# A quad's partial sums kept in one PSUM bank and copied out by ScalarE, instead of added on VectorE

## The chip, the cores and the metric

The kernel runs on one core of a Trainium2 chip. The metric is the device time of one execution in microseconds (us). The engines are TensorE (PE in the rows, its weight loads PEld), VectorE (DVE), ScalarE (ACT), GpSimd (POOL) and SyncE (SP, which issues the loads and stores).

## The reference

Three blocks follow one another on a sequence of 768 tokens, 2 batches and 512 features, all in fp32:

```python
state = gamma * state + einsum(k[t], v[t]);  y[t] = scale * einsum(q[t], state)
u  = x + (xt @ U @ V).T;      x2 = u + relu(u @ w_ch1) @ w_ch2
h  = relu(x2 @ w_in);         u, v = split(h);   v_n = layernorm(v)
out = (u * (w_spatial @ v_n + b)) @ w_out
```

The first block is a linear attention with decay (8 heads of 64), the second a low-rank token mix and an MLP of width 2048, the third a gated MLP of width 1024 with a 768 x 768 mix over tokens.

## The kernel before, in words

Every fp32 operand is split into two fp32r tiles, a high and a low part, and each product of two operands is three matmuls (`triple`, L640). The stages, by the time of the profile: attention and token mix up to about 70 us; the first MLP up to about 322 us, in eight steps of two hidden tiles (its first two steps by plain products, tiles `c`, the other six by quads), whose second products go to tiles `acc`; the gate half of the third block (`gate_u`, quads `qu`) to 345 us; its value half with the norm (`gate_v`, quads `qv`) to 381 us; the token mix (tiles `pz`) to 427 us; the output product (`final`, quads `qo`) to 457 us.

A **quad** (L653) computes a 2 x 2 block product by seven products instead of eight. `PRODUCTS` (L320) names their operands 1 to 7; sums and differences of operands (`s1`, `t1` and so on) are made beforehand. Each of the seven is two triples, that is six matmuls, of 384 columns (first MLP, `gate_u`) or 256 columns (`gate_v`, `final`). With P1 to P7 for the products, the four outputs are

```
out00 = P1 + P2             out10 = P1 + P6 + P7 + P4
out01 = P1 + P6 + P5 + P3   out11 = P1 + P6 + P7 + P5
```

There are 28 quads: 12 in the first MLP (m = 2 to 7, two batches, tiles `q20` to `q71`), 4 `qu`, 6 `qv` and 6 `qo`. Before, a quad takes four PSUM banks of the eight: `qa` collects P1 and then P2, `qb` P6, `qc` P7 and then P4, `qd` P5 and then P3. P1 is copied to an SBUF tile y1 (L667, shown as L457, on ScalarE or VectorE), VectorE adds P6 to it (L668) and makes y2 = P7 + y1 (L670). `store` then adds y1 or y2 to the bank for three of the outputs, on VectorE (L730, L769, L786 or L849), and takes out00 straight from `qa`. In the first MLP `store` goes on with a relu on ScalarE (L731), the high part (L732) and the low part (L733).

No order is written out by hand. Each operation goes to a planner (`Plan`, L44) with a key, its dependences, its tiles and its cost on each engine that may take it (`aps`, `vps` and others, from L263). The planner fills the engines' queues by time (`arrange`, L93); for PE it takes what can start first. The only instruction it does not cost is the load of ScalarE's function table, which is put ahead of the first square root of the norm (L797). PE, VectorE and ScalarE each run their own queue in order.

A matmul that writes a bank anew, or adds to it, waits until the reads of that bank that stand before it are done. In the rows a wait shows as idle time ahead of the instruction, of PEld in PE's case.

## Time and profile before

| what | value |
|---|---|
| median of 3 runs | 462.59 us (462.5 to 462.69) |
| span of the profiled execution, first to last instruction | 460.2 us |
| granted TensorE clock over it | 1.000 |
| PE / VectorE / ScalarE / POOL busy | 455.8 / 408.6 / 258.1 / 104.1 us |
| DMA, mean | 94 GB/s |

The profiled execution is given by its span alone; no total of its own is listed. The span lies 2.4 us under the median of the runs. Busy times are sums over the span; whether an engine's idle time costs anything is seen in the waits and in the timeline.

### The profile page before, as it was taken

The numbers are of one execution on the slowest core, as the hardware profiler recorded it, in microseconds if no ns is written. First come the engines' busy times: TensorE is split into PE (matmuls) and PEld (weight loads), VectorE is DVE, ScalarE is ACT, GpSimd is POOL, SyncE is SP. The second block draws the span as 40 slices with busy tenths as digits, with TensorE's granted clock in tenths as the row PEclk, the third lists the DMA queues.
The fourth block names the chain that finished last, engine by engine and source line by source line (L and its number), as shares of the span: only waits on it lengthen the run. The fifth ranks groups of instructions, "written<-read, shape, count | busy, mean of one in ns | idle before, by whom it ended". The sixth has DMA issues, their size and how long they took to land.

```text
span 460.2 us, 8518 instructions
## 1 busy us (share of the span) xinstructions
PE 455.8 (99%) x3258; PEld 446.2 (97%) x3258; DVE 408.6 (89%) x867; ACT 258.1 (56%) x532; POOL 104.1 (23%) x99
## 2 busy tenths in 40 slices
PE   9999999999999999999999999999999999999997
PEld 6898899999999999999999999999999999999997
DVE  2969999999999999999789788899998899989943
ACT  3667676475556656566355444557657878443410
POOL 3164333433323221321131012101310001240000
PEclk9999999999999999999999999999999999999999
DMA  8996212141422233334112112100004220000042
GB/s 309 399 400 240 93 45 93 32 153 47 136 94 91 93 93 108 120 93 139 46 58 81 47 46 70 35 1 0 2 0 139 93 91 1 1 2 1 0 180 95
DMA packets 14727, 43.34 MB, mean 94 GB/s; under 512 B 1760, under 2 KB 2400, under 8 KB 14688
## 3 DMA queue, kind: packets, MB, share of 16 engines
q1 hardware_dynamic: 14544, 42.80, 27.0%
q8 instruction: 25, 0.41, 0.4%
q14 instruction: 14, 0.11, 0.1%
q10 hardware_dynamic: 144, 0.02, 0.0%
HBM read 39.67 MB, written 3.15 MB: 93 GB/s over the span
## 4 chain that ended last, share of the span: by engine, by line
PE 99%; DVE 0%; issue 0%
PE acc L336 29%; PE pz L336 11%; PE c L336 7%; PE x L336 5%; PE sc L336 3%; PE g L336 1%; PE t L470 1%; PE ds L336 1%; PE idle L336 1%; PE hu L336 1%; PE qu11c L336 0%; PE q40a L336 0%; PE qu11d L336 0%; PE qu11a L336 0%; PE qu01d L336 0%; PE qu01c L336 0%
## 5 line engine op out<-in xcount | busy, mean ns | idle before, releaser
L336 PE MATMUL acc<-a,hw 128*128 128x384 f32 x512 | 130.2, 334 | 0.0
L336 PEld LDWEIGHTS acc<-a,hw 128*128 128x128 f32 x512 | 92.5, 188 | 0.3 <-DVE a L733 0.3
L336 PE MATMUL acc<-a,lw 128*128 128x384 f32 x256 | 85.5, 334 | 0.0
L758 DVE TENSOR_TENSOR x<-acc,x 128x384 f32<-128x384 f32 x128 | 69.6, 550 | 7.0 <-PE acc L336 6.8
L565 POOL TENSOR_TENSOR rw<-rw,tw 128x512 int32<-128x512 int32 x32 | 43.9, 1374 | 112.7 <-DVE rw L564 102.1
L336 PEld LDWEIGHTS acc<-a,lw 128*128 128x128 f32 x256 | 48.1, 188 | 0.0
L731 ACT ACTIVATE y<-y 128x384 f32<-128x384 f32 x36 | 18.9, 524 | 39.3 <-DVE y L730 39.2
L561 ACT ACTIVATE yw<-raww 128x512 f32<-128x512 f32 x32 | 21.6, 678 | 16.7 <-DVE rw L564 16.6
L564 DVE SCALAR_TENSOR_TENSOR rw<-yw,rw 128x512 uint32<-128x512 uint32 x32 | 24.2, 759 | 0.0
L733 DVE TENSOR_TENSOR a<-y,a 128x384 fp32r<-128x384 f32 x36 | 21.0, 585 | 2.7 <-ACT a L732 2.4
L562 ACT ACTIVATE tw<-raww 128x512 int32<-128x512 uint32 x32 | 21.5, 673 | 2.0 <-POOL rw L565 2.0
L422 DVE SCALAR_TENSOR_TENSOR pt<-sc,scales,shared 128x384 f32<-128x384 f32 x21 | 11.9, 611 | 8.3 <-PE sc L336 8.2
L732 ACT CAST a<-y 128x384 fp32r<-128x384 f32 x36 | 18.5, 514 | 1.1
L336 PE MATMUL pz<-hws,vn 128*128 128x384 f32 x72 | 19.1, 335 | 0.0
L336 PE MATMUL pz<-ws,vn 128*128 128x384 f32 x108 | 19.0, 334 | 0.0
L336 PEld LDWEIGHTS pz<-ws,vn 128*128 128x128 f32 x108 | 18.8, 188 | 0.0
L563 DVE TENSOR_SCALAR rw<-yw 128x512 uint32<-128x512 uint32 x32 | 18.3, 582 | 0.1
L565 POOL TENSOR_TENSOR rwo<-rwo,two 128x512 int32<-128x512 int32 x4 | 5.2, 1294 | 54.8 <-DVE rwo L564 54.8
L574 DVE TENSOR_TENSOR lw<-rw,hw 128x512 fp32r<-128x512 f32 x20 | 17.1, 855 | 0.0
L336 PE MATMUL c<-f00b,hw 128*128 128x384 f32 x64 | 16.4, 338 | 0.0
L336 PE MATMUL c<-f01b,hw 128*128 128x384 f32 x64 | 16.2, 334 | 0.0
L573 ACT CAST hw<-rw 128x512 fp32r<-128x512 f32 x20 | 12.4, 619 | 6.2 <-POOL rw L565 5.8
(1090 smaller groups left out, 1293.8 us busy)
## 6 DMA issues: line engine op xcount, KB each, us to landing
raww<-in_w SPq DMA_DIRECT2D x32, 512.0 KB, 3.5
q<-in_qT SPq DMA_DIRECT2D x8, 384.0 KB, 8.0
k<-in_kT SPq DMA_DIRECT2D x8, 384.0 KB, 8.0
kk<-in_k SPq DMA_DIRECT2D x8, 384.0 KB, 8.0
v<-in_v SPq DMA_DIRECT2D x8, 384.0 KB, 7.9
out_y<-out SPq DMA_DIRECT2D x11, 256.0 KB, 2.1
raws<-in_ws SPq DMA_DIRECT2D x6, 384.0 KB, 2.9
rawwu<-in_wu SPq DMA_DIRECT2D x4, 512.0 KB, 3.8
```

The lines of the kernel that those rows point to most:

```text
L336: nc.tensor.matmul(o, l, r, start=start, stop=stop, skip_group_check=True)
L561: op({"A": c}, lambda E: E.activation(y.t, words(1).bitcast(F32), AF.Copy, scale=2.0 ** -112), r=whole, w=[y])
L562: op({"A": c}, lambda E: E.activation(t.t, words(0), AF.Copy, scale=2.0 ** -29), r=whole, w=[t])
L563: op({"V": vone(n)}, lambda E: E.tensor_single_scalar(r.t, y.t.bitcast(U32), 3, ALU.logical_shift_left), r=[y], w=[r])
L564: op({"V": vss(n)}, lambda E: E.scalar_tensor_tensor(r.t, y.t.bitcast(U32), 0x80000000, r.t, ALU.bitwise_and, ALU.bitwise_or), r=[y, r], w ...
L565: op({"G": gss(n)}, lambda E: E.tensor_tensor(r.t.bitcast(I32), r.t.bitcast(I32), t.t, ALU.add), r=[r, t], w=[r])
L573: op({"A": acp(DM)}, lambda E: E.copy(h.t, f(r.t)), r=[r], w=[h])
L574: op({"V": vss(DM), "G": gss(DM)}, lambda E: E.tensor_sub(l.t, f(r.t), f(h.t)), r=[r, h], w=[l])
L731: op({"A": (525, False)}, lambda E: E.activation(y[0](), y[0](), AF.Relu), r=[y[1]], w=[y[1]])
L732: op({"A": acp(T)}, lambda E: E.copy(t.t[:, 0, :], y[0]()), r=[y[1]], w=[(t, 0)])
L733: op({"V": vss(T), "G": gss(T)}, lambda E: E.tensor_sub(t.t[:, 1, :], y[0](), f(t.t[:, 0, :])), r=[y[1], (t, 0)], w=[(t, 1)])
L758: op({"V": vps(T)}, lambda E, o=o, v=xs(b, d, h): E.tensor_add(v, o.t, v), r=[o, ("X", b, d, h)], w=[("X", b, d, h)])
```

## The change

The seven products are put in the order 1 2 6 5 7 4 3 (they stood in the order 1 5 6 7 2 4 3). Products 1, 6, 7 and 4 all go to `qa`, one on top of the other, so that the bank holds P1, then P1 + P6, then P1 + P6 + P7, then out10. After each of the first three ScalarE copies the bank to an SBUF tile (y for 1, 6 and 7; the first of them may also go to VectorE). Product 2 has `qb`, products 5 and 3 have `qd`; `qc` is gone. `store` adds y(1) to `qb`, y(7) and y(6) to `qd`; out10 needs no addition and is read from `qa`. Where `ys2` gives two SBUF tiles (256 columns), the copy of 7 takes the tile of the copy of 1.

```diff
--- before.py
+++ after.py
@@ -305,7 +305,7 @@
 STEP0, STEP1, UV = 5.0, 5.0, 20.0
 LOADS = "q0 k0 q1 k1 U V0 q2 k2 V1 q3 k3 w10 w11 q4 k4 w20 w21 q5 k5 q6 k6 q7 k7".split()
 LEAD = 10.0
-ORDER = '1567243'
+ORDER = '1265743'
 LAST = "b11 b21 t1=b12-b11 t1 t2=b22-t1 t2 t3=b22-b12 t3 t4=b21-t2 t4 b22"
 LASTSUMS = "t1=b12-b11 t1 t2=b22-t1 t2 t3=b22-b12 t3 t4=b21-t2 t4"
 SUM0, SUM1 = 80.0, 80.0
@@ -655,27 +655,22 @@
 
 
 
-        qa, qb, qc, qd = (bank([P, n], f"q{name}{x}") for x in "abcd")
-        y1, y2, y3 = ys()
-        done = set()
+        qa, qb, qd = (bank([P, n], f"q{name}{x}") for x in "abd")
+        ys = dict(zip("167", ys()))
         for x in order:
             plan.key += STEP[n] * plan.pace
-            done.add(x)
-            product({"1": qa, "6": qb, "7": qc, "5": qd, "2": qa, "4": qc, "3": qd}[x], PRODUCTS[x], x in "1675")
-            if x == "1":
-                op({"A": aps(n), "V": vps(n)}, lambda E: cpy(E, y1[0](), qa.t), r=[qa], w=[y1[1]])
-            elif x == "6":
-                op({"V": vps(n)}, lambda E: E.tensor_add(y1[0](), qb.t, y1[0]()), r=[qb, y1[1]], w=[y1[1]])
-            elif x == "7":
-                op({"V": vps(n)}, lambda E: E.tensor_add(y2[0](), qc.t, y1[0]()), r=[qc, y1[1]], w=[y2[1]])
-            elif x == "2":
-                store(0, 0, qa)
+            product({"1": qa, "6": qa, "7": qa, "4": qa, "2": qb, "5": qd, "3": qd}[x], PRODUCTS[x], x in "125")
+            if x in ys:
+                y = ys[x]
+                op({"A": aps(n), "V": vps(n)} if x == "1" else {"A": aps(n)}, lambda E, y=y: cpy(E, y[0](), qa.t), r=[qa], w=[y[1]])
+            if x == "2":
+                store(0, 0, qb, ys["1"], ys["1"])
             elif x == "4":
-                store(1, 0, qc, y1, y3)
+                store(1, 0, qa)
             elif x == "3":
-                store(0, 1, qd, y1, y1)
-            if x in "57" and {"5", "7"} <= done:
-                store(1, 1, qd, y2, y2)
+                store(0, 1, qd, ys["6"], ys["6"])
+            if x == "7":
+                store(1, 1, qd, ys["7"], ys["7"])
 
     def ys3(name):
         def get():
@@ -686,7 +681,7 @@
     def ys2(name):
         def get():
             bs = [Buf("st", [P, DM // 2], F32, f"y{name}{x}") for x in range(2)]
-            return [(lambda z=z: bs[z].t[:], bs[z]) for z in (0, 1, 1)]
+            return [(lambda z=z: bs[z].t[:], bs[z]) for z in (0, 1, 0)]
         return get
 
     def own(x):
```

The planner makes new queues of this. The three places below are quoted with the semaphores waited for in brackets (`Activation` is ScalarE's).

**PE, a quad of the first MLP** (`q40`; `acc` are the second products of the step before). Before, ahead of product 4 (the rows `q40c<-...qw`): one product of the other bank and one `acc`.

```order
L336 MATMUL q40a<-f00b_722,hw14a 128x384
L336 MATMUL q40a<-f00b_722,lw14a 128x384
L336 MATMUL q40a<-f00b_733,hw14a 128x384 x2
L336 MATMUL q40a<-f00b_733,lw14a 128x384
L336 MATMUL acc_2580<-a_2480,hw_1960 128x384 [waits DVE_49]
L336 MATMUL acc_2580<-a_2480,hw_1960 128x384
L336 MATMUL acc_2580<-a_2480,lw_1992 128x384
L336 MATMUL acc_2580<-a_2406,hw_1990 128x384 x2
L336 MATMUL acc_2580<-a_2406,lw_2004 128x384
L336 MATMUL q40c<-f00t_1266,qw_2121 128x384 [waits DVE_49]
L336 MATMUL q40c<-f00t_1266,qw_2121 128x384 x2
L336 MATMUL q40c<-f00t_1316,qw_2121 128x384 x3
```

Now, from the last rows of product 7 (`hsbw`, `lsbw`) to product 4 (`qw`), both in `q40a`:

```order
L336 MATMUL q40a<-f00t_1228,lsbw_2147 128x384
L336 MATMUL q40a<-f00t_979,hsbw_2137 128x384 x2
L336 MATMUL q40a<-f00t_979,lsbw_2147 128x384
L336 MATMUL acc_2586<-a_2489,hw_1946 128x384 x2
L336 MATMUL acc_2586<-a_2489,lw_1958 128x384
L336 MATMUL acc_2586<-a_2435,hw_1994 128x384 x2
L336 MATMUL acc_2586<-a_2435,lw_2008 128x384
L336 MATMUL q40a<-f00t_1264,qw_2091 128x384 [waits Activation_49]
L336 MATMUL q40a<-f00t_1264,qw_2091 128x384 x2
L336 MATMUL q40a<-f00t_1416,qw_2091 128x384 x3
L336 MATMUL acc_2609<-a_2489,hw_1946 128x384 [waits DVE_49]
L336 MATMUL acc_2609<-a_2489,hw_1946 128x384
```

Product 4 stood three groups of six matmuls behind product 7 (an `acc`, product 2, an `acc`) and waited for VectorE; it stands one group behind it and waits for ScalarE.

**PE, the last quad of the program** (`qo12`, 256 columns). Before, product 7 (end of it), product 2 and the start of product 4:

```order
L336 MATMUL qo12c<-lsbwo_5267,f21t_5369 128x256
L336 MATMUL qo12c<-hsbwo_5257,f21t_5369 128x256
L336 MATMUL qo12a<-hwo0a,f21b_5177 128x256 [waits Activation_49]
L336 MATMUL qo12a<-lwo0a,f21b_5177 128x256
L336 MATMUL qo12a<-hwo0a,f21b_5177 128x256
L336 MATMUL qo12a<-hwo1a,f21b_5208 128x256
L336 MATMUL qo12a<-lwo1a,f21b_5208 128x256
L336 MATMUL qo12a<-hwo1a,f21b_5208 128x256
L336 MATMUL qo12c<-qwo_4988,f21t_5362 128x256 [waits DVE_49]
L336 MATMUL qo12c<-qwo_4988,f21t_5362 128x256 x2
```

Now, product 7, product 4 and the start of product 3:

```order
L336 MATMUL qo12a<-hsbwo_5008,f21t_5307 128x256 [waits Activation_49]
L336 MATMUL qo12a<-lsbwo_5017,f21t_5307 128x256
L336 MATMUL qo12a<-hsbwo_5008,f21t_5307 128x256
L336 MATMUL qo12a<-hsbwo_5236,f21t_5354 128x256
L336 MATMUL qo12a<-lsbwo_5245,f21t_5354 128x256
L336 MATMUL qo12a<-hsbwo_5236,f21t_5354 128x256
L336 MATMUL qo12a<-qwo_4966,f21t_5347 128x256 [waits Activation_49]
L336 MATMUL qo12a<-qwo_4966,f21t_5347 128x256 x2
L336 MATMUL qo12a<-qwo_5173,f21t_5383 128x256 x3
L336 MATMUL qo12d<-hsbwo_5008,f21b_5286 128x256 [waits DVE_49]
L336 MATMUL qo12d<-lsbwo_5017,f21b_5286 128x256
```

Product 4 follows product 7 in the same bank with nothing between them.

**ScalarE, the second quad of `gate_v`** (`qv01`). Before, around the load of the function table:

```order
L457 COPY yv_4361<-qv01a 128x256 [waits PE_49,Activation_49]
L787 ACTIVATE r_4339<-qv00d 128x256 [waits DVE_49]
L635 CAST hws_4375<-raws_4321 128x384 [waits DMAHW3_49]
L635 CAST ws_4382<-raws_4321 128x384
L797 ACT_TABLE_LOAD
L797 ACTIVATE sm_4359<-sm_4359 128x2 [waits DVE_49]
L635 CAST ws_4401<-raws_4348 128x384 [waits DMAHW4_49]
L787 ACTIVATE r_4409<-qv01a 128x256 [waits PE_49]
L787 ACTIVATE r_4419<-yv_4399 128x256 [waits DVE_49]
```

Now:

```order
L782 ACTIVATE r_4344<-qv00d 128x256 [waits DVE_49]
L782 ACTIVATE r_4381<-qv01b 128x256 [waits DVE_49]
L457 COPY yv_4388<-qv01a 128x256 [waits PE_49]
L457 COPY yv_4398<-qv02a 128x256 [waits PE_49,Activation_49]
L792 ACT_TABLE_LOAD
L792 ACTIVATE sm_4359<-sm_4359 128x2 [waits DVE_49]
L457 COPY yv_4337<-qv01a 128x256 [waits PE_49]
L782 ACTIVATE r_4420<-yv_4337 128x256 [waits DVE_49]
L782 ACTIVATE r_4426<-qv02b 128x256 [waits DVE_49]
```

The first row `yv<-qv01a` here is the copy after product 6, the second the copy after product 7; the table load and the square root stand ahead of the second. On PE, the six matmuls of `qv02b` stand between product 7 of `qv01` and product 4, which waits for that copy:

```order
L336 MATMUL qv01a<-lsbwv_4194,f10t_3935 128x256
L336 MATMUL qv01a<-hsbwv_4183,f10t_3935 128x256
L336 MATMUL qv02b<-hwv0a,f10b_3722 128x256
L336 MATMUL qv02b<-lwv0a,f10b_3722 128x256
L336 MATMUL qv02b<-hwv0a,f10b_3722 128x256
L336 MATMUL qv02b<-hwv1a,f10b_3744 128x256
L336 MATMUL qv02b<-lwv1a,f10b_3744 128x256
L336 MATMUL qv02b<-hwv1a,f10b_3744 128x256
L336 MATMUL qv01a<-qwv_3750,f10t_3899 128x256 [waits Activation_49]
L336 MATMUL qv01a<-qwv_3750,f10t_3899 128x256 x2
L336 MATMUL qv01a<-qwv_4036,f10t_3941 128x256 x3
```

Before, the next copy of a bank behind the square root was that of `qv02a`, five rows later; now the copy that product 4 waits for stands directly behind it.

## Rows read from the trace of the kernel before

**Rows 1.** The page, part 1: busy time, share of the span, instructions.

```profile
PE 455.8 (99%) x3258; PEld 446.2 (97%) x3258; DVE 408.6 (89%) x867; ACT 258.1 (56%) x532; POOL 104.1 (23%) x99
```

**Rows 2.** Windows: stretch, us, busy (instructions) of five engines, clock, DMA.

```profile
70.00:123.00 53.00, 53.00 (x308) 53.00 (x307) 52.08 (x99) 30.86 (x60) 20.73 (x17) 1.00 0.25 82
123.00:312.00 189.00, 188.97 (x1090) 188.65 (x1089) 173.64 (x344) 104.72 (x201) 38.36 (x29) 1.00 0.25 79
312.00:345.00 33.00, 33.00 (x194) 33.00 (x193) 32.08 (x67) 19.86 (x44) 7.29 (x7) 1.00 0.00 1
345.00:381.00 36.00, 36.00 (x285) 36.00 (x285) 31.72 (x107) 28.24 (x72) 0.00 (x0) 1.00 0.32 104
...
424.00:457.00 33.00, 33.00 (x267) 32.77 (x265) 21.99 (x52) 8.91 (x22) 0.00 (x0) 1.00 0.22 84
```

**Rows 3.** Waits of the weight loads: total us, times, longest us.

```profile
PEld t L470 <- DVE x L454: 0.9, 3, 0.5
...
PEld acc L336 <- DVE a L733: 0.3, 1, 0.3
```

**Rows 4.** Chain by time: start us, us, what; two stretches.

```profile
288.10 1.04 PE acc L336 x6
...
442.42 0.72 PE qo10d L336 x6
...
455.50 0.78 PE qo12c L336 x6
```

**Rows 5.** One line's instructions: min/median/max ns, first and last start.

```profile
L668 DVE TENSOR_TENSOR y<-q50b,y x1: 558/558/558, 221.6 to 221.6; 128x384 f32<-128x384 f32 x1
...
L670 DVE TENSOR_TENSOR yv<-qv00c,yv x1: 418/418/418, 349.5 to 349.5; 128x256 f32<-128x256 f32 x1
...
L457 ACT COPY y<-q61a x1: 482/482/482, 264.2 to 264.2; 128x384 f32<-128x384 f32 x1
...
L457 ACT COPY yv<-qv01a x1: 373/373/373, 352.2 to 352.2; 128x256 f32<-128x256 f32 x1
```

**Rows 6.** Timeline, last quad: start us, us, engine, instruction, idle before.

```profile
452.34 0.28 PE L336 MATMUL qo12a<-hwo1a,f21b 128*128 128x256 f32 x1
...
452.66 0.37 ACT L457 COPY yo<-qo12a 128x256 f32<-128x256 f32 x1 [1.85 <-PE qo12a L336]
...
454.50 0.28 PE L336 MATMUL qo12c<-hsbwo,f21t 128*128 128x256 f32 x1
...
454.82 0.43 DVE L670 TENSOR_TENSOR yo<-qo12c,yo 128x256 f32<-128x256 f32 x1 [0.23 <-PE qo12c L336]
...
455.30 0.78 PEld L336 LDWEIGHTS qo12c<-qwo,f21t 128*128 128x128 f32 x6
```

**Rows 7.** Timeline, a first-MLP quad.

```profile
263.84 0.33 PE L336 MATMUL q61a<-f01b,lw16a 128*128 128x384 f32 x1
...
264.21 0.48 ACT L457 COPY y<-q61a 128x384 f32<-128x384 f32 x1 [0.94 <-PE q61a L336]
```

**Rows 8.** Timeline around 184 us.

```profile
183.88 0.56 DVE L733 TENSOR_TENSOR a<-y,a 128x384 fp32r<-128x384 f32 x1
...
184.50 0.19 PEld L336 LDWEIGHTS acc<-a,hw 128*128 128x128 f32 x1 [0.35 <-DVE a L733]
```

**Rows 9.** Timeline of ScalarE, the gated MLP's table load.

```profile
353.16 0.53 ACT L635 CAST ws<-raws 128x384 fp32r<-128x384 f32 x1
353.70 1.28 ACT L797 ACT_TABLE_LOAD   x1
355.00 0.21 ACT L797 ACTIVATE sm<-sm 128x2 f32<-128x2 f32 x1
355.11 0.50 ACT L635 CAST ws<-raws 128x384 fp32r<-128x384 f32 x1
```

**Rows 10.** Waits of all engines: total us, times, longest us.

```profile
ACT yw L561 <- DVE rw L564: 16.6, 16, 2.4
```

## The prediction

> **What bounds the kernel now.** I read the page's first part, then the windows by stage, then the waits of PE, and the timeline where one engine hands over to another. PE is busy for 455.8 us of the span of 460.2 [rows 1], but that share alone proves little, since matmul ends are modelled. The windows say more: from 70 us to the end of the matmuls at 457 us PE is busy in every microsecond but 0.03 of each stage shown, at a clock of 1.00, while VectorE is nearly full in some (52.08 of 53 us) and ScalarE half full [rows 2]. The pace says it best. Six matmuls of 384 columns take 1.04 us and six of 256 take 0.72, wherever VectorE is full or not [rows 4], so a triple costs 0.52 or 0.36 us and nothing waits behind it. The waits of the weight loads on other engines are small; the only one behind the first 70 us is 0.3 us, once [rows 3]. PE sets the end. The change issues the same matmuls, so all it can give back is what PE still loses, and all that it can take is new waits of PE.
>
> **What it removes.** Two additions per quad on VectorE, L668 and L670: 16 quads x 2 x 0.55 us (the row of 384 columns reads 558 ns, others slightly less) = 17.6, and 12 x 2 x 0.42 = 10.1, together 27.7 us [rows 5]. VectorE lies beside PE, so on the path this is worth nothing by itself; two losses of PE go with it. At 184 us a low part L733 ended at 184.44 and PE's weight load came 0.06 later, about 0.3 us late [rows 8]; with VectorE relieved I count half, -0.15 (bounds -0.3 and 0). And four of the last quads wait for L670 to free `qc`, each like the row shown: 0.78 us for six matmuls in place of 0.72 [rows 4, 6]; -0.24.
>
> **What it adds.** Copies of a bank on ScalarE: 80 in place of 27 (of the 28 first copies, four now go to VectorE), 32 x 0.48 + 21 x 0.37 = 23.2 us more [rows 5]. ScalarE has the room, 258.1 us of 460.2 [rows 1]; what costs is that PE now waits for these copies before it may go on with the same bank. The price of such a handoff comes from rows. With 256 columns: last matmul starts at 452.34, copy at 452.66 (ScalarE had been idle), 0.37 us long [rows 6]; then 0.05 us to PE's weight load, as behind L670 (454.82 + 0.43 = 455.25, load at 455.30). Start to weight load 0.74. With 384 columns: 263.84 to 264.21, and 0.48 of copy [rows 7], and 0.05: 0.90. An unhindered weight load starts with the matmul ahead of it, so six matmuls in between cover 0.72 or 1.04 us, and none cover nothing. A late load costs about what it is late, less 0.02 (0.08 late, 0.06 lost [rows 6]).
>
> By the new order of PE the handoffs fall so:
>
> - **Last quad.** Product 4 stands directly behind product 7: 0.74 late, +0.72 us. Nothing hides it; no other work is left. Product 3 behind it waits for VectorE's addition, which starts from the same copy and is done while product 4 runs. The seven other handoffs of `final` that have six matmuls between them miss by 0.02 each if ScalarE is idle: +0.1 (0 to 0.4). With the -0.24 above the final stage comes to +0.6.
> - **Second quad of `gate_v`.** ScalarE's queue has the copy of `qv02a`'s first product, the table load, a square root, and then the copy that product 4 of `qv01` waits for. Call S the start of the last matmul of product 7. The last matmul of `qv02a`'s product started at S - 0.72, so its copy runs from S - 0.40 to S - 0.03. The table load starts when the instruction ahead has ended and takes 1.28 us, the square root follows 0.02 later, and the next one 0.11 after that starts [rows 9]: the copy starts at S + 1.38, ends at 1.75, and PE's load comes at 1.80. It was due at S + 0.72. +1.0 us (bounds 0.6, if `qv02a` runs earlier, and 1.5, if the square root must wait for VectorE's statistics). Before, only casts stood behind the load, and PE did not notice it.
> - **Rest of `gate_v` and `gate_u`.** ScalarE is busy 28.24 of 36 us from 345 us on [rows 2] and gets ten more copies, 3.7 us, which makes 89%. Five more handoffs have only six matmuls between; the others nine or more. I take +0.5 (0 to 2).
> - **First MLP, 12 quads.** Products 1 and 6, and 6 and 7, have 18 matmuls between them; product 4 has six behind product 7: 1.04 against 0.90, so the copy may start 0.14 us late. In eight of the twelve, three or four conversions of weights stand between the copies of 6 and 7, some of which wait for VectorE or POOL. Such waits of ScalarE are seen now: 16 of them, 1.04 us in the mean [rows 10]. From the end of product 6 to that of product 7 there are 4.16 us, and ScalarE has about 3 us of work in them, so a wait of the mean size just fits. Lower bound 0; upper bound 8 x (1.04 - 0.14) = 7.2. I take 0.6, near the lower end, since the rows show PE missing one handoff in all these stages today.
> - Attention, the token mix and the plain products keep their instructions: 0.
>
> **The sum.** +0.6 + 1.0 + 0.5 + 0.6 - 0.15 = +2.55 us. The profiled execution has a span of 460.2 and the runs a median of 462.59; I keep the 2.4 us around it. 462.6 + 2.5 = **465.1 us**.
>
> A rule of the Trainium skill speaks against this change. "Perfetto Trace Analysis", section "Optimizing Tensor Performance", says that independent groups of matmuls should rotate through different PSUM banks, so that one bank is read out while the next is filled. Taken alone it would charge every handoff from 7 to 4 at its full price; the next part works that out from rows; the trace before has no handoff without matmuls between to hold against it.
>
> **The rivals.**
>
> - **Only what cannot be covered is paid, and the table load is not met** (ScalarE reaches it earlier than its place says). Sum: +0.6 - 0.3 = 462.9 us. For it: the copies are few and ScalarE idles for 44%. Against: the place in the queue. 0.15.
> - **Faster: VectorE paces PE after all.** Place: 70 to 220 us, where it is full [rows 2]. If a tenth of the 27.7 us came back to PE, the time would be 462.6 - 2.8 + 1.6 (last quad, table load) = 461.4 us; it decides if more than 2.5 us come back. Against it: the same 1.04 us per six matmuls where VectorE is less than full. 0.05. The Trainium skill, same page, section "Optimizing Scalar/DVE Operations", says that moving work to ScalarE may make sense where VectorE is saturated; the condition holds in the trace, but PE's idle time there does not show a gain to have.
> - **ScalarE's queue misses many handoffs.** The eight quads of the first MLP pay the mean wait: +7.2 in place of 0.6, 471 us. For it: in-order queue, conversions ahead of the copies. Against: PE met nearly all its handoffs so far. 0.12.
> - **One bank leaves no cover at all.** All 28 handoffs from 7 to 4 at the full price, 16 x 0.88 + 12 x 0.72 = 22.7, in place of the 0.72 of the last quad: about 487 us. That is what the rule would make of it; the order shows other banks' matmuls between in 27 of 28. 0.02.
> - That the change does not do what it says is excluded by the order: 55 rows fewer on VectorE, 53 more on ScalarE.
>
> **The numbers.** My forecast, slower by 0.9 to 5 us, has 0.66. A measurement of this kernel tells about 0.2% (0.93 us) from no change. Slower by more: 0.66 + 0.12 + 0.02, less 0.02 for its lower edge, 0.78. Within: 0.15 + 0.02 = 0.17. Faster: 0.05. The range takes in the bounds of the terms and part of the third rival: from 463.0 (only the unavoidable waits) to 468.5.
>
> **What would show it.** PE's waits should name L457 of ScalarE: one of about 0.7 us in `qo12a` near the end, one of about 1 us in `qv01a` some 352 to 360 us into the span, and short ones on `q..a`. PE's busy time should stay within 1 us of 455.8, VectorE fall to about 382, ScalarE rise to about 281. A PE without waits on ScalarE, or a pace of six matmuls other than 1.04 and 0.72 us, would prove me wrong.

## The result, and the profile after

The changed kernel takes 469.24 us in the median of four runs (468.37 to 469.94), the kernel before 462.54 beside it: ratio 1.015, interval 1.0137 to 1.0162, 6.7 us slower. I had said 465.1 and a range up to 468.5: the sign was right, the size was not. The profiled execution has a span of 467.5 us, 7.3 more than before. Three of the four executions had a mean granted clock of 0.996, the fourth (468.37 us) 1.000.

Page of the changed kernel, part 1 (answers to [rows 1]):

```profile
PE 458.7 (98%) x3258; PEld 447.6 (96%) x3258; DVE 388.6 (83%) x813; ACT 277.0 (59%) x585; POOL 107.9 (23%) x100
```

VectorE fell by 20.0 us and ScalarE rose by 18.9, each less than I had worked out (27.7 and 23.2). PE is busy 2.9 us longer with the same matmuls; it was slower somewhere. Its waits, as [rows 3] (total us, times, longest us):

```profile
PEld t L470 <- DVE x L454: 1.7, 3, 1.3
...
PEld acc L336 <- DVE a L728: 1.2, 1, 1.2
PEld qv01a L336 <- ACT yv L457: 1.1, 1, 1.1
PEld q21a L336 <- ACT y L457: 1.1, 1, 1.1
...
PEld qo12a L336 <- ACT yo L457: 0.7, 1, 0.7
PEld c L336 <- DVE lw L574: 0.6, 1, 0.6
...
PEld qo00a L336 <- ACT yo L457: 0.5, 1, 0.5
...
PEld q31a L336 <- ACT y L457: 0.4, 1, 0.4
```

Five waits are on the copies (L457), the kind foreseen, and three on VectorE at places where no instruction was changed: the attention's transposes, a plain product `c`, an `acc`. The windows from 62 to 72 us show the rest (columns as [rows 2]; the number behind the five busy times is the granted clock):

```profile
62.00:66.00 4.00, 2.86 (x30) 2.26 (x28) 4.00 (x8) 1.70 (x3) 1.40 (x1) 1.00 0.00 0
66.00:68.00 2.00, 1.70 (x10) 1.38 (x10) 2.00 (x5) 1.93 (x4) 1.43 (x1) 0.89 0.03 8
68.00:70.00 2.00, 2.00 (x9) 2.00 (x8) 2.00 (x6) 1.29 (x3) 0.24 (x1) 0.50 0.79 246
70.00:72.00 2.00, 2.00 (x14) 2.00 (x13) 0.53 (x1) 0.36 (x2) 1.28 (x1) 0.76 0.80 184
```

PE stood idle for 1.1 of four us and 0.3 of the next two, and then ran at half clock (0.50, the level of 1.2 GHz) from 67.6 to about 71.0 us. The timeline says why it stood (start us, us, engine, line, instruction):

```profile
62.68 1.40 POOL L565 TENSOR_TENSOR rw<-rw,tw 128x512 int32<-128x512 int32 x1 [0.99 <-DVE rw L564]
62.85 1.64 DVE L528 TENSOR_TENSOR f01b<-x,f01b 128x384 fp32r<-128x384 f32 x1
...
64.42 0.54 DVE L723 SCALAR_TENSOR_TENSOR a<-c,a 128x384 fp32r<-128x384 f32 x1
64.89 1.01 DVE L454 TENSOR_TENSOR x<-x,shared 128x384 f32<-128x384 f32 x2
65.48 0.31 PEld L470 LDWEIGHTS t<-shared,x 128*128 128x128 f32 x3 [1.33 <-DVE x L454]
```

In the kernel before the same stretch of the timeline reads:

```profile
63.70 0.56 DVE L454 TENSOR_TENSOR x<-x,shared 128x384 f32<-128x384 f32 x1
...
64.31 0.31 PEld L470 LDWEIGHTS t<-shared,x 128*128 128x128 f32 x3 [0.16 <-DVE x L454]
...
66.04 0.55 DVE L528 TENSOR_TENSOR f01b<-x,f01b 128x384 fp32r<-128x384 f32 x1
```

The planner had put L528, a low part that in the kernel before ran at 66.04 with nobody waiting for it, ahead of the two products L454 that the transposes wait for, and it ran beside a POOL instruction for 1.64 us in place of 0.55.

**Where the 7.3 us lie**, by the start of the same matmul in both timelines: the first quad `q20a` starts 2.93 later (122.25, now 125.18; the matmuls `x<-q,s` just ahead of the first wait start at 62.93 in both); `q21a` adds 1.0 at 151 us, `q31a` 0.4 at 183; the stall of [rows 8] is gone, -0.3; `acc` adds 1.1 at 322, `qv01a` 1.1 at 361, the last stage 1.0 (`qo00a` 0.5, `qo12a` 0.7, four handoffs of [rows 6] that no longer miss, -0.26). The last product starts at 463.43 in place of 456.12.

### The profile page after: what moved, and what is told of

Read it like the earlier page. It is cut to its first block, busy times and chain, and to the rows that moved or that the text cites. A ratio compares the mean times of both kernels' runs of the same rounds, so it can differ in the third digit from the quotient of the medians.

```text
span 467.5 us, 8481 instructions
## 1 busy us (share of the span) xinstructions
PE 458.7 (98%) x3258; PEld 447.6 (96%) x3258; DVE 388.6 (83%) x813; ACT 277.0 (59%) x585; POOL 107.9 (23%) x100
## 4 chain that ended last, share of the span: by engine, by line
PE 71%; DVE 24%; ACT 3%; issue 1%; ACTq 0%
PE acc L336 21%; PE c L336 6%; PE x L336 4%; DVE x L753 3%; PE sc L336 3%; DVE a L728 2%; PE g L336 2%; DVE pz L831 1%; DVE x L832 1%; PE ds L336 1%; PE t L470 1%; DVE lw L574 1%; PE idle L336 1%; DVE y L725 1%; DVE rw L564 1%
## 5 line engine op out<-in xcount | busy, mean ns | idle before, releaser
L726 ACT ACTIVATE y<-y 128x384 f32<-128x384 f32 x36 | 18.9, 524 | 21.1 <-DVE y L725 20.5
L728 DVE TENSOR_TENSOR a<-y,a 128x384 fp32r<-128x384 f32 x36 | 24.5, 682 | 4.9 <-ACT a L727 4.6
L564 DVE SCALAR_TENSOR_TENSOR rw<-yw,rw 128x512 uint32<-128x512 uint32 x32 | 21.6, 682 | 0.0
L336 PE MATMUL pz<-hws,vn 128*128 128x384 f32 x72 | 18.9, 334 | 0.0
L574 DVE TENSOR_TENSOR lw<-rw,hw 128x512 fp32r<-128x512 f32 x20 | 15.7, 784 | 0.3 <-ACT hw L573 0.3
L722 ACT ACTIVATE a<-c 128x384 fp32r<-128x384 f32 x16 | 7.8, 490 | 10.8 <-PE c L336 7.2
L563 DVE TENSOR_SCALAR rw<-yw 128x512 uint32<-128x512 uint32 x32 | 14.1, 458 | 0.0
```

What stands on the lines that cost most here:

```text
L336: nc.tensor.matmul(o, l, r, start=start, stop=stop, skip_group_check=True)
L563: op({"V": vone(n)}, lambda E: E.tensor_single_scalar(r.t, y.t.bitcast(U32), 3, ALU.logical_shift_left), r=[y], w=[r])
L564: op({"V": vss(n)}, lambda E: E.scalar_tensor_tensor(r.t, y.t.bitcast(U32), 0x80000000, r.t, ALU.bitwise_and, ALU.bitwise_or), r=[y, r], w ...
L574: op({"V": vss(DM), "G": gss(DM)}, lambda E: E.tensor_sub(l.t, f(r.t), f(h.t)), r=[r, h], w=[l])
L726: op({"A": (525, False)}, lambda E: E.activation(y[0](), y[0](), AF.Relu), r=[y[1]], w=[y[1]])
L728: op({"V": vss(T), "G": gss(T)}, lambda E: E.tensor_sub(t.t[:, 1, :], y[0](), f(t.t[:, 0, :])), r=[y[1], (t, 0)], w=[(t, 1)])
```

## The experiments

In most of them single operations are moved in the finished plan. `find` names one by its engine and tiles; `put` and `behind` give it a start just after (or before) another's, and what depends on it follows. All else stays as planned. What an expectation calls its theory is the outcome that the account so far asks for, its rival the outcome that would speak against it. Ratios are to the kernel before on the same chip (461.8 to 462.1 us in these runs).

### The early stall and the clock

The matmuls `x<-q,s` start between 62.69 and 63.81 us in the traces of this section and the next two, a spread that lies ahead of the waits and the fall of the clock. So the start of `q20a` is given from them too: 59.32 us behind them in the kernel before, 62.25 in the changed one.

**early_moved**: one instruction of VectorE moved back.

```diff
+        put(find("V", "f01b120"), find("V", "x71", "shared"), 0.5)
```

> The changed kernel with one instruction of VectorE moved: the low part of f01b12 (L528), which ran for 1.64 us beside a POOL instruction at 62.85 us, stands behind the two L454 products that PE's transposes wait for instead of ahead of them. Theory (planner's new order of VectorE's queue starves PE, and the clock falls after it): PE's wait for x at L470 goes from 1.3 us to under 0.5, the wait for lw at L574 goes or shrinks, the granted clock from 66 to 72 us is 1.00 in place of 0.50 to 0.89; 3 to 4 us less, so a span of about 463.5 to 464.5 and a ratio to the kernel before of 1.007 to 1.009. Rival (all of the 7 us is ScalarE's hand-overs behind 70 us, and the early stall only shifts idle time): the stall goes, the span stays within 1 us of 467.5, ratio 1.014 to 1.016.

Ratio 1.0129 (1.0114 to 1.0145), span 465.7. The wait at L470 is back to 0.4, the clock at 1.00, but PE now comes earlier to the low part `lw` and waits 1.1 us for it in place of 0.6: L564 still stands ahead of L574. `q20a` starts at 123.42, 60.23 behind `x<-q,s`: 2.0 us less than in the changed kernel, where the theory had 3 to 4. The rival falls.

**early_filled**: the wait stays, but PE is given something to do.

```diff
             def run(_, tr=tr, h=h):
+                for _ in range(7 if (i, h) == (7, 0) else 0):
+                    mm(tr.t.rearrange("p c t -> p (c t)"), warm[:, 0:P], warm, True, True)
                 for c in range(TC):
```

> The changed kernel with seven extra bf16 matmuls of 384 columns ahead of the transposes of the last attention tile, written to the bank that the transposes then overwrite; VectorE's order and PE's wait for it stay. Theory (the clock falls because PE stood idle, and costs by itself about 1.9 us): the transposes still start as late as before the edit, but the granted clock from 66 to 72 us stays near 1.00 and the matmuls keep to 0.17 us; 1.5 to 2 us less than the changed kernel, ratio 1.011 to 1.012. Rival (the slow stretch is something else than the clock's answer to PE's idle time, such as the port of weights): still 0.32 us per matmul for some 4 us, ratio 1.015 or more.

Ratio 1.0129 (1.0116 to 1.0143). The transposes start where they did (timeline), and the clock stays (windows):

```profile
64.21 1.33 PE L336 MATMUL t<-const-bfloat16-1.0 128*128 128x384 bf16 x7
...
65.42 1.01 PE L472 MATMUL t<-shared,x 128*128 128x128 f32 x6
```

```profile
66.00:68.00 2.00, 1.70 (x10) 1.38 (x11) 2.00 (x5) 1.99 (x4) 1.49 (x1) 1.00 0.00 0
68.00:70.00 2.00, 2.00 (x17) 2.00 (x16) 2.00 (x6) 1.20 (x2) 0.18 (x1) 1.00 0.85 262
```

`q20a` starts at 123.57, 60.71 behind `x<-q,s`, 1.5 us less than in the changed kernel; all four executions have a clock of 1.000. So the halved clock is an answer to PE's idle time, with a price of its own of about 1.5 us.

**before_early**: the kernel before with L528 moved the other way.

```diff
+        put(find("V", "f01b120"), find("V", "c0010", "a0001"), -0.5)
```

> The kernel before with the one instruction moved the other way: the low part of f01b12 (L528) stands ahead of the second L728 and of the two L454 products instead of some 3 us later; banks, sums and all else are those of before. Theory (the place of this instruction alone makes the early loss, with the new scheme of the quads or without): PE waits 1 us or more for x at L470, and if PE's idle time is then as long as in the changed kernel the granted clock falls to about half for some 4 us; 1 to 4 us more than before, ratio 1.002 to 1.009. Rival (the loss comes with the chain of one bank): the same as before within 0.2%.

Ratio 1.0024 (1.0014 to 1.0035); PE waits 1.2 us at L470 and none for `lw`; all seven executions at a clock of 0.999 or 1.000. The place of one instruction costs 1 us in the old scheme too; this wait alone did not bring the clock down.

**before_hole**: the kernel before with VectorE's order of the changed kernel there, so that PE waits twice.

```diff
+        behind(find("V", "yw20 rw20"), find("V", "c0010 a0001"), -3.0)
+        behind(find("V", "f01b120"), find("V", "c0010 a0001"), -2.0)
+        behind(find("V", "yw20 rw20", 1), find("V", "x71 shared"), 1.0)
```

> The kernel before with VectorE's order of the changed kernel near 65 us, as in before_early, and with a conversion (L564) ahead of the low part lw (L574) as well, so that PE waits twice within 3 us; banks and sums are those of before. Theory (the fall of the clock comes from PE's two waits close together, in whatever scheme): waits of 1.2 us for x and about 0.6 us for lw; in a part of the executions the granted clock is 0.989 to 0.996 and the time 2 to 10 us longer than in the others, which lie 1.4 us above before; ratio 1.003 to 1.02. Rival (the fall belongs to the new scheme): every execution at a clock of 0.999 or 1.000, ratio 1.002 to 1.004.

Ratio 1.0048 (1.0032 to 1.0063). Three executions lie at 463.2 to 463.5 us with a clock of 1.000, three at 465.0 to 465.3 with 0.996; the profiled one is of these. Its windows and waits:

```profile
66.00:68.00 2.00, 1.70 (x10) 1.22 (x9) 2.00 (x5) 1.71 (x4) 1.21 (x1) 0.86 0.03 8
68.00:70.00 2.00, 2.00 (x7) 2.00 (x7) 2.00 (x5) 0.28 (x1) 0.46 (x1) 0.50 0.63 211
```

```profile
PEld t L470 <- DVE x L454: 2.0, 3, 1.6
...
PEld c L336 <- DVE lw L574: 0.6, 1, 0.6
```

The early loss and the fall of the clock need neither the new banks nor the new sums: the old scheme pays both once VectorE's queue stands like that.

### The hand-overs: ScalarE's queue

**table_first**: the function table of the square root loaded at the start.

```diff
-        op({"A": (1500.0, False)}, lambda e: e.activation(psm.tile([P, 1], F32, name="table"), warm[:, 0:1], AF.Copy))
+        op({"A": (1500.0, False)}, lambda e: e.activation(psm.tile([P, 1], F32, name="table"), warm[:, 0:1], AF.Sqrt))
```

> The changed kernel with the dummy activation at the start made a square root, so that the one table that is loaded there serves the whole program and none is loaded at 360.7 us; the order of everything else stays. Theory (the 1.28 us of the table load stand ahead of the copy that qv01a waits for): PE's wait of 1.1 us for yv goes wholly, 0.9 to 1.0 us less, span about 466.5, ratio 1.012 to 1.014. Rival (the copy waits for VectorE's statistics behind the square root as well): the copy starts as late, nothing is gained, ratio 1.015.

Ratio 1.0123 (1.0103 to 1.0142), span 467.0. The changed kernel has at this place:

```profile
360.68 1.28 ACT L792 ACT_TABLE_LOAD   x1
...
361.97 0.21 ACT L792 ACTIVATE sm<-sm 128x2 f32<-128x2 f32 x1
362.08 0.35 ACT L457 COPY yv<-qv01a 128x256 f32<-128x256 f32 x1
...
362.49 0.19 PEld L336 LDWEIGHTS qv01a<-qwv,f10t 128*128 128x128 f32 x1 [1.06 <-ACT yv L457]
```

Without the load product 4 of `qv01` waits for nothing. But in this execution a cast (L635) waited for its load of `ws` until 359.19, with the copy after product 6 behind it, and product 7 waited 0.7 us. The table load was the cause in the changed kernel; the same quad meets another instruction where that one is gone.

**scalar_moved**: the copies PE waits for moved ahead of what held them up, at four places; with the table at the start.

```diff
+        behind(find("A", "raww28 yw28"), find("A", "q21a y212"), 1.0)
+        behind(find("A", "raww112 yw112"), find("A", "q31a y312"), 1.0)
+        last = find("A", "qv01a yv010")
+        behind(find("A", "sm00"), last, 1.0)
+        behind(find("A", "raws5 ws15"), last, 2.0)
+        behind(find("A", "s21t3 f21t30"), find("A", "qo00a yo000"), 1.0)
```

The first of these, in the trace of the changed kernel: a conversion that waits for VectorE stands ahead of the copy.

```profile
150.99 0.66 ACT L561 ACTIVATE yw<-raww 128x512 f32<-128x512 f32 x1 [1.56 <-DVE rw L564]
...
151.56 0.46 ACT L457 COPY y<-q21a 128x384 f32<-128x384 f32 x1
...
152.07 0.47 PEld L336 LDWEIGHTS q21a<-f01t,qw 128*128 128x128 f32 x3 [1.05 <-ACT y L457]
```

> The changed kernel with ScalarE's queue alone mended: in four places the copy of a bank that PE waits for stands ahead of the instruction that held it up (two conversions L561 at 151 and 183 us, a square root and a cast of a late load near 361 us, a cast at 434 us), and the table is loaded at the start. Theory (these four hand-overs cost 1.0, 0.4, 1.1 and 0.5 us and nothing else hangs on them): PE's waits on L457 in q21a, q31a, qv01a and qo00a go, that of 0.7 in qo12a stays; 2.9 us less than the changed kernel, span about 464.6, ratio 1.008 to 1.010. Rival (ScalarE is too full there, and what is put back is missed by VectorE, POOL and then PE): half of it or less, ratio 1.012 or more.

Ratio 1.0119 (1.0076 to 1.0161); span 464.1 at a clock of 0.999. All four waits are gone, and three new ones stand there: `qo01a` 0.4 and `q30a` 0.3 on L457, `qv01d` 0.3 on VectorE. Against the 466.1 of **after_again** (below; same chip, clock 1.000) it is 2.0 us, two thirds of what was expected. The ratio is higher than that because two of the six executions, with clocks of 0.993 and 0.989, had spans of 470.3 and 472.9; the two waits near 65 us stand in this kernel as well.

**vector_moved**: VectorE alone mended, near 65 us and at 322 us.

```diff
+        low = find("V", "rw11 hw11 lw11")
+        behind(find("V", "f01b120"), low, 1.0)
+        behind(find("V", "yw20 rw20", 1), low, 2.0)
+        behind(find("V", "y711 a7101"), find("V", "s10t1 s10t2", 1), -1.0)
```

> The changed kernel with three instructions of VectorE moved and nothing else: the low part of f01b12 (L528) and the second half of a weight conversion (L564) stand behind the low part lw (L574) near 65 us, and the low part L728 that the wait of 1.2 us at 322 us names stands ahead of the sums of the next operands. Theory (of the 7.3 us, VectorE's new order costs 2.9 near 65 us and 1.1 at 322 us): the waits for x, lw and a go, the clock stays at 1.00, 3.9 us less than the changed kernel, span 463.3 to 463.9, ratio to the kernel before 1.006 to 1.008. Rival (the instructions that were put back make PE wait somewhere else): one of these waits comes back under another name, 2 us less or fewer, ratio 1.010 or more.

Ratio 1.0103 (1.009 to 1.0116), span 464.8, clock 1.000 in each execution. The three waits are gone; 0.6 us in `c` (on L498) and 0.8 in `qu00a` (on a copy, L457) came in their place. The last was hidden behind the wait of `acc`: in the changed kernel the same copy stands behind the same instructions of ScalarE and ends at 330.12, 0.28 us ahead of PE's load; here PE, which no longer waits at `acc`, wants to load at 326.76, and the copy ends at 327.49.

**all_moved**: both edits and the table at the start, and at the end the last product of `qo11` put between products 7 and 4 of `qo12`.

```diff
+        for z in range(2):
+            behind(find("P", f"hsbwo{z} lsbwo{z} f21b22{z} qo11d"), find("P", "hsbwo1 lsbwo1 f21t31 qo12a"), 10.0 + z)
```

> Both edits together, and in the last stage the last product of the quad before stands between products 7 and 4 of the last quad. Theory (the scheme with one bank costs nothing by itself; all of the loss is order): all waits that the change brought go, span 459.7 to 460.3, ratio 0.998 to 1.001. Rival (one bank leaves too little room, some hand-overs are late however the queues stand): 1 us or more stays, ratio 1.002 or more.

Ratio 1.0062 (1.005 to 1.0074). 3 us stay. The theory falls here. Of the 3.3 us of the profiled span, 0.6 lie ahead of 63 us (`x<-q,s` at 63.57); the rest is in waits at new places: `qu00a` 0.7, `c` 0.6, and 0.3 each in `q30a`, `qv01d`, `qo01a` and `qo12d`.

**after_again**: the changed kernel itself, beside them.

> The changed kernel as it is, beside the three others on the same chip: ratio 1.014 to 1.016, the same waits at the same places and the same fall of the clock from 67 to 71 us.

The profiled execution had a clock of 1.000, the waits as named, and a span of 466.1; `q20a` started at 123.68, so the waits near 65 us are worth 1.4 of the 2.9 us and the clock 1.5. The other five executions had clocks of 0.989 to 0.995 and spans of 471.3 to 474.0, which gives the ratio of 1.0231 (1.019 to 1.0271): a miss of the expectation. The clock has only a part in it: an estimate from these rows, the share below full clock times the span, gives 2.4 to 5.2 us, and the spans are 5.2 to 7.9 us over 466.1 (for the profiled fall, from the windows, it gives 1.7, and 1.5 was measured). What the rest is no run shows.

**all_moved2**: six more moves, each for a wait in the trace of all_moved.

```diff
+        add = find("V", "hu71")
+        behind(find("V", "s00t3 f00t31"), add, 1.0)
+        behind(find("V", "s00t1", 1), add, 2.0)
+        behind(find("A", "raww110 yw110"), find("A", "q30a y301"), 1.0)
+        copy = find("A", "qu00a yu001")
+        behind(find("A", "s11t1 f11t11"), copy, 1.0)
+        behind(find("A", "s11t3 f11t30"), copy, 2.0)
+        behind(find("A", "f11b221"), copy, 3.0)
+        behind(find("V", "sm00", 3), find("V", "qv02b yv020"), 1.0)
+        copy = find("A", "qo01a yo010")
+        behind(find("A", "s21t4 f21t40"), copy, 1.0)
+        behind(find("A", "s21t3 f21t31"), copy, 2.0)
+        behind(find("V", "qo11d yo111 out111"), find("V", "qo12d yo120 out121"), 1.0)
```

> The run all_moved with six more moves, each for a wait that its trace shows: two instructions of VectorE that nobody needs soon stand behind the additions L498 (wait of 0.6 us in c), a conversion behind the copy of q30a (0.3), three casts behind the second copy of qu00a (0.7), the row of small statistics behind the additions L781 (0.3, qv01d), two casts behind the first copy of qo01a (0.4), and the addition for qo12d ahead of that for qo11d (0.3). Theory (one bank costs nothing that order cannot give back): these waits go, 2.5 to 3 us less than all_moved, ratio 0.999 to 1.002. Rival (with one bank per quad some hand-over is always late, and what is mended moves the wait to the next): less than 1.5 us, ratio 1.003 or more.

Ratio 1.0068 (1.0056 to 1.008): nothing gained over all_moved. The rival was right; new waits took the place of those mended:

```profile
PEld qu10a L336 <- ACT yu L457: 1.0, 2, 0.7
...
PEld qv02a L336 <- ACT yv L457: 0.8, 1, 0.8
PEld c L336 <- DVE f01b L528: 0.5, 1, 0.5
...
PEld qo01a L336 <- ACT yo L457: 0.4, 1, 0.4
PEld q30a L336 <- ACT y L457: 0.3, 1, 0.3
```

### The hand-overs: cover on PE

If mending ScalarE's queue only moves the wait, too little may stand between two products of one bank on PE. **cover_400**, **cover_450**, **cover_600**: the planner is told that a copy takes 0.40, 0.45 or 0.60 us longer, and plans anew (here 0.45). In cover_400 and cover_600 the table is loaded at the start, and what stands ahead of `lw` on VectorE near 65 us (`f01b120`, a second `yw20 rw20`, two low parts of `xtok`) is put behind it.

```diff
-                op({"A": aps(n), "V": vps(n)} if x == "1" else {"A": aps(n)}, lambda E, y=y: ...
+                op({e: (c[0] + 450.0, c[1]) for e, c in ({"A": aps(n), "V": vps(n)} if x == "1" else {"A": aps(n)}).items()}, lambda E, y=y: ...
```

> The changed kernel, planned anew with each copy of a bank costed 0.4 us longer than before, so that the planner puts more matmuls of others between two products of one bank: of the 84 places 10 had only 0.71 us of matmuls and 24 about 1.04; now 1 has 0.71 and 13 about 1.04 to 1.4, and the last quad's product 4 still stands directly behind 7. Near 65 us the low part lw (L574) stands ahead of what held it up, and the table is loaded at the start. Theory (PE's waits on L457 come from too little cover, not from any one instruction in ScalarE's queue): all waits on L457 but the 0.7 in qo12a go or stay under 0.3, ratio 1.002 to 1.004. Rival (what costs is that any new order of VectorE's and ScalarE's queues meets PE somewhere): waits on other lines in their place, ratio 1.006 or more.

Ratio 1.0078 (1.0061 to 1.0094). From 75 us on PE waits twice, 0.4 us in `acc` and 0.7 in `qo12a`: no copy is late but the one with nothing ahead of it. The time is lost at 66 us, where the transposes' followers `g` wait 2.6 us for a low part that my own move in the early stage had put back, and the clock falls (0.996 in three of six executions).

> As cover_400 with 0.6 us: another plan with as much cover (none of the 84 places under 1.04 us but the last). Theory (cover): as cover_400, ratio 1.002 to 1.004. Rival (any new order costs): waits at other places than in cover_400, on lines other than L457, ratio 1.006 or more.

Ratio 1.0081 (1.0068 to 1.0094). Here `qo00a` waits 1.5 us on its copy and `pz` 0.9 in two places. More cover does not help where the plan fails elsewhere; this run speaks for the rival.

> The changed kernel, planned anew with each copy of a bank costed 0.45 us longer, and nothing else: no instruction moved by hand, the table as in the changed kernel. VectorE's order near 65 us is that of the changed kernel, so its two waits there stay. Theory (cover): behind 70 us PE waits on L457 in qo12a alone (0.7), the two early waits and in a part of the executions the fall of the clock stay; 3.5 to 4 us less than the changed kernel, ratio 1.004 to 1.008. Rival (any new order of the queues costs): further waits of 0.3 us or more behind 70 us, 2 us or more together, ratio 1.009 or more.

Ratio 1.0076 (1.0062 to 1.0089), as the theory had it, with no operation moved by hand. The stage of the 12 quads that had lost 1.0 and 0.4 us is full (windows):

```profile
123.00:312.00 189.00, 189.00 (x1092) 189.00 (x1091) 163.00 (x317) 116.28 (x225) 42.81 (x33) 1.00 0.26 78
312.00:345.00 33.00, 33.00 (x194) 33.00 (x193) 29.22 (x62) 23.03 (x53) 9.11 (x8) 1.00 0.02 8
```

What is lost lies ahead of it (the two waits near 65 us, at a clock of 0.999 or 1.000 in all five executions) and behind it, in `gate_v` (`qv02a` 0.5) and the last stage (`qo00a` 0.6, `qo12a` 0.7); of these the theory had `qo12a` alone.

But it is not the matmuls between that made the first MLP full. Nine matmuls stand between products 7 and 4 there (1.56 us) in place of six (1.04), and the copy does not need them: in eleven of the 12 quads it starts 0.37 us behind the start of product 7's last matmul, as behind an idle ScalarE [rows 7], in the twelfth 0.53. The changed kernel had 1.59 in `q21a` and 0.95 in `q31a`. In `q21a`, where the last matmul starts at 148.94 (timeline):

```profile
149.31 0.48 ACT L457 COPY y<-q21a 128x384 f32<-128x384 f32 x1
...
150.50 1.05 PEld L336 LDWEIGHTS q21a<-f01t,qw 128*128 128x128 f32 x6
```

The copy ends at 149.79; with six matmuls between, PE's load would have been due at 149.98. The new plan, then, gave the copy its place on ScalarE. scalar_moved did the same for `q21a` and `q31a` by hand, with six matmuls between as before.

**cover_best**: the plan of cover_450 with moves near 65 us, two more near 73 us, the table at the start, and the end as in all_moved.

```diff
+        low = find("V", "rw11 hw11 lw11")
+        behind(find("V", "f01b120"), low, 1.0)
+        behind(find("V", "yw20 rw20", 1), low, 2.0)
+        add = find("V", "f01b221")
+        behind(find("V", "s00t3 f00t31"), add, 1.0)
+        behind(find("V", "s00t1", 1), find("V", "c0011 a0011"), 1.0)
+        for z in range(2):
+            behind(find("P", f"hsbwo{z} lsbwo{z} f21b22{z} qo11d"), find("P", "hsbwo1 lsbwo1 f21t31 qo12a"), 10.0 + z)
+        behind(find("V", "qo11d yo111 out111"), find("V", "qo12d yo120 out121"), 1.0)
```

> The plan of cover_450 with the early stage and the end mended: near 65 us two instructions of VectorE stand behind the low part lw (as in vector_moved) and two more behind the work that PE waits for near 73 us; at the end the last product of the quad before stands between products 7 and 4 of the last quad; the table is loaded at the start. Theory (one bank costs next to nothing where each hand-over has 1.4 us of other matmuls and no early wait is made): no wait of the change stays over 0.4 us, ratio 0.999 to 1.002. Rival (some of the 3 us that stayed in all_moved2 belongs to the scheme whatever its cover): ratio 1.004 or more.

Ratio 1.0036 (1.0024 to 1.0049), between theory and rival: the best of the new scheme, still slower than before. Windows:

```profile
123.00:312.00 189.00, 189.00 (x1092) 189.00 (x1091) 163.22 (x317) 116.69 (x226) 42.95 (x34) 1.00 0.25 78
312.00:345.00 33.00, 33.00 (x196) 33.00 (x195) 28.38 (x60) 22.63 (x52) 8.54 (x8) 1.00 0.06 18
345.00:381.00 36.00, 36.00 (x280) 36.00 (x279) 26.57 (x89) 26.94 (x72) 0.00 (x0) 1.00 0.26 80
381.00:424.00 43.00, 43.00 (x254) 43.00 (x253) 42.07 (x96) 24.35 (x53) 15.86 (x16) 1.00 0.04 12
424.00:458.00 34.00, 33.57 (x269) 33.02 (x267) 20.05 (x46) 12.80 (x32) 2.62 (x2) 1.00 0.19 70
```

For 301 us, with 22 of the 28 quads, PE loses nothing. What stays is 0.7 us up to `q20a`, of which 0.3 lie ahead of `x<-q,s`, and 0.9 in the last stage.

**cover_best2**: two casts in the last stage put behind the copies that PE waits for.

```diff
+        behind(find("A", "s21t3 f21t30"), find("A", "qo00a yo000"), 1.0)
+        behind(find("A", "s21t4 f21t41"), find("A", "qo01a yo011"), 1.0)
```

> cover_best with two casts of ScalarE moved behind the copies that qo00a and qo01a wait for near 428 and 435 us; the rest as it is. Theory (what stayed in cover_best is order too, 0.6 and 0.2 us, and the wait of 0.4 us for lw at 90 us): 0.8 us less than cover_best, ratio 1.000 to 1.003. Rival (a wait moves on, as it did from all_moved to all_moved2): ratio as cover_best, 1.003 to 1.005.

Ratio 1.0038 (1.0024 to 1.0051): the wait in `qo00a` went, and `qo01a` (0.4), `qo00d` (0.4) and `qo02a` (0.2) took it over. Whether the last stage can be ordered without a loss is open.

## Why the prediction was wrong

- **The step that failed: "Attention, the token mix and the plain products keep their instructions: 0".** They keep them, in another order. 2.9 of the 7.3 us lie there, all ahead of the first quad: 1.4 of waits (after_again, at a clock of 1.000) and 1.5 of clock (early_filled). [Rows 3] had the warning: of PE's waits on other engines the largest was that on L454. A place without slack, in a kernel whose planner reorders every queue, needed its order read and a bound. before_hole shows that this part belongs to no bank.
- **First MLP, VectorE: no term.** My term for this stage counted late copies of ScalarE and took VectorE as relieved. At 322 us PE waits for VectorE, and that cost 1.1. PE and VectorE there (timeline):

```profile
319.51 0.51 ACT L727 CAST a<-y 128x384 fp32r<-128x384 f32 x1
...
322.12 0.34 PE L336 MATMUL acc<-a,hw 128*128 128x384 f32 x1
...
322.72 0.55 DVE L728 TENSOR_TENSOR a<-y,a 128x384 fp32r<-128x384 f32 x1
...
323.32 0.19 PEld L336 LDWEIGHTS acc<-a,hw 128*128 128x128 f32 x1 [1.19 <-DVE a L728]
```

  The input of L728 was ready at 320.02, but five other instructions stood ahead of it on VectorE from 320.38 on. The same five stand there in the kernel before, where PE did not wait:

```profile
314.36 0.51 ACT L732 CAST a<-y 128x384 fp32r<-128x384 f32 x1
...
317.31 0.55 DVE L733 TENSOR_TENSOR a<-y,a 128x384 fp32r<-128x384 f32 x1
```

  So the order at this place is old, and what is new is that VectorE comes to it late. Counted from the first matmul of `qu00a` (312.90 before, 316.87 now), PE comes to this `acc` at 5.2 us in both kernels; the cast starts at 1.46 before and 2.64 now, the low part at 4.41 and 5.85. vector_moved, which puts L728 ahead of these sums, takes the wait away, but 0.8 of it comes back in `qu00a`. Why VectorE is behind there no run shows.
- **Last quad, +0.6 for the stage:** `qo12a` waited 0.7 as priced, the four old misses went. `qo00a` (0.5) was not foreseen: the stage came to 1.0.
- **Table load, +1.0:** 1.1, with the rows in the order and nearly the times worked out (copy 1.45 us behind the last matmul of product 7; I had 1.38).
- **Rest of the gates, +0.5:** 0.1.
- **First MLP, copies, +0.6 (0 to 7.2):** 1.4 in two quads, `q21` and `q31`, each by the mechanism named: a conversion ahead of the copy, waiting for VectorE.
- **Stall at 184 us, -0.15:** -0.3, the whole of it.

My terms came to 2.55, and what they stand for measured 3.3, which alone would have given about 466 us, well inside the range. The step costed at nothing (2.9) and the wait that had no term (1.1) made the rest; neither had a bound in the range. The relief of VectorE bought the 0.3 us at 184 us at most, as argued: PE's windows were full before.

The rule that I had weighed (the Trainium skill, "Perfetto Trace Analysis", section "Optimizing Tensor Performance") says that independent groups of matmuls should rotate through different banks, so that reading one out overlaps the matmuls of the next. The runs bear it out only where nothing stands between: product 4 directly behind 7 cost 0.7. Of the 84 places of the changed kernel where a product follows another in its bank, 29 have 0.7 to 1.1 us of other matmuls between, and 26 of these were in time to within 0.1 us. The three late ones (`q21a`, `q31a`, `qv01a`) had a conversion or the table load ahead of the copy, and `qo00a` was late with 1.4 us between. In cover_best 22 quads cost nothing, in one bank each. Keeping one bank was not the loss by itself; what the hand-overs lost came from copies that ScalarE's queue held up and, in the last quad, from a hand-over with nothing between. Whether the new scheme can be ordered without any loss stays open: its best run is 1.7 us slower than the kernel before.

## What to carry to other kernels

Where a planner makes the queues, "its instructions do not change" is no reason for a zero: read the new order at every place where the old profile shows the bounding engine waiting, and bound what you do not read. When a reused buffer makes a hand-over, look at what stands ahead of it in the queue of the engine that frees the buffer, and not only at the work that covers it. Here 0.45 us more on each copy in the planner's costs gave a plan that lost nothing in the first MLP; moving single instructions gave back a part (2.0 of 2.9 us in scalar_moved) and passed the rest on (all_moved2 gained nothing over all_moved).

## What the runs showed of the hardware

- **Short idle times of PE can cost more than their length.** In the kernels whose profiled execution has two waits near 65 us (1.3 and 0.6 us in the changed kernel) 15 of 32 executions had a mean clock of 0.996 or less (the changed kernel, after_again, table_first, scalar_moved, before_hole, cover_450). In 43 executions with one of them, none, or the first filled, none had less than 0.998; with one wait of 2.6 us (cover_400) three of six had 0.996. It is not the same each time: none of five in cover_450, five of six in after_again. The profiled fall cost 1.5 us. Seven executions of after_again and scalar_moved, all on one chip, had clocks of 0.989 to 0.995 and spans 5 to 9 us over that of the profiled one; where in the span their clock fell, and what made the part that it does not account for, no profile shows.
- **VectorE behind POOL.** L528 took 1.64 us beside a POOL instruction that ended at 64.08, and ended itself 0.41 later; alone it takes 0.55. The Trainium skill, "SBUF — State Buffer", section "SBUF: two separate sides", says that a GpSimd instruction that reads SBUF and a VectorE instruction with two SBUF inputs take a shared port in turns, each for its whole length. The trace agrees (0.41 us behind the end of the POOL instruction, against 0.55 alone). An instruction with a single SBUF input was held up in the same way: in before_hole L563 took 1.25 us from 63.00, beside a POOL instruction that ended at 63.96, and it takes 0.42 alone.
